# Banded attention and a gated MLP on one core: values of two head pairs in one place, a load moved behind stores, a third row buffer

## The chip, the cores and the metric

The kernel runs on one core of a Trainium2 chip. The metric is the device time of one execution in microseconds. Three runs of the kernel before took 677.02, 677.27 and 681.09 us; the median is 677.27. Engine names follow the profile: PE is TensorE (PEld its weight loads), DVE is VectorE, ACT is ScalarE, POOL is GpSimd, SP is SyncE, which here only issues DMAs.

## What is computed

```python
def _attn_ref(q, k, v, n_global, n_local):          # q, k, v: (4, 8, 768, 64) float32
    scores = np.matmul(q, k.transpose(0, 1, 3, 2)) / np.sqrt(D)
    rel = pos[:, None] - pos[None, :]
    is_global = pos[None, :] < n_global             # 8
    is_local = (rel >= 0) & (rel < n_local)         # 96
    dist = np.where(is_global & ~is_local, float(n_local), np.abs(rel))
    scores = scores - slopes[:, None, None] * dist  # one slope per head
    scores = np.where(is_global | is_local, scores, -1e9)
    a = softmax(scores)
    return np.matmul(a, v)

def _moe_ref(x, w_in, w_out):                       # x: the attention's output, (3072, 512); w_in (512, 2048)
    h = x @ w_in
    return (h * np.clip(h + 3.0, 0.0, 6.0) / 6.0) @ w_out
```

Each query sees at most 96 local and 8 global keys, so only a band of the scores is ever computed. All is float32 at float32 accuracy: the large products are made of three products of rounded parts (high by high, low by high, high by low).

## The kernel before, in words

The 3072 rows are eight **blocks** of 384 rows (4 batches by two halves of the sequence), each of three row tiles of 128. For each block the attention of 8 heads is made in four **pairs** of heads, and then the MLP: for each of 16 slices f of the hidden layer a first product (`first`, L164, 12 matmuls into a PSUM bank `hp`), the gate (L175 on ACT, L176 on DVE), its split into a high part `gh` (L182 on POOL) and a low part `gl` (L189 on DVE), and a second product (`second`, L196, 9 matmuls into three banks `acc`). PE alternates between the two, so a slice is two **half-steps** of some 2.1 us each; `halves` (L430) hands control back after each, and the caller then puts the attention's work of that half-step in between.

Blocks 0 and 1 are made in an earlier stage, in which the weights are decoded too. From block 2 on there is the main loop (L549): while block i goes through the MLP, the attention of block i + 1 is made, by a list of `units`, one per half-step, which `attention` (L577) writes out. For pair p, from unit 6p on, it holds:

- units 0 to 2: `scores` of the three row tiles (L767, four matmuls each into a bank `sp` or `tp` in turn; then DVE L774 and ACT's exponential L778);
- unit 3: the sums (L786, L787), and `normalize` of two tiles on POOL (L796); unit 4: the third tile;
- units 4 and 5: `spread`, which transposes on DVE (L821) and stores to a DRAM tile `there` (L823), and `fetch`, which reads that back as the tile `weights` (L830);
- units 3 to 5: `split` of the next pair's queries and keys into rounded parts: `q1` on ACT (L740), `kx` on POOL (L741) and on DVE (L747), `q2` on DVE (L744). Its step 2 ends with a load of a later pair's keys and queries (`load_next`, L295);
- unit 11, thus five half-steps behind the next pair's first scores: `values` (L848), 24 or 20 matmuls of 64 columns into a bank `xp`, a copy and a subtraction out of it (L150 on ACT, L151 on DVE) into the block's x, and a load of a later pair's values.

In block 2, the first of the main loop, all units stand one half-step later, and the first pair (12) is split ahead of the loop; the load that this split ends with stands on SP between the stores of block 0 and those of block 1.

After a block's last slice, `store` (L50) copies the three accumulators on ACT into tiles `o` (L53) and stores each (L54 on SP). The pool of `o` has two tiles in the main loop. Block 1's accumulators are the banks named sp, tp and xp.

Order: the instructions of PE, SP and POOL are held to the order of the program (`in_order`, L567); on ACT and DVE the framework's own scheduler sets the order.

Of the kernel before, what the change touches and what calls it, by code (L numbers as in the profile page):

```python
# [21 lines left out]
TB = NT * P  # L22
# [34 lines left out]
class Kernel:  # L57
# [229 lines left out]
    def load(self, n, values):  # L287


        if n < len(self.blocks) * NPAIR:  # L290
            parts = [(slice(KW + QW, LOAD), slice(None))] if values else [(slice(0, KW + QW), slice(None))]
            if n < EARLY and not values:
                parts = [(slice(0, KW), slice(None))] + [(slice(KW + j * TB, KW + (j + 1) * TB), slice(j * D, (j + 1) * D)) for j in range(2)]
            for columns, rows in parts:
                self.nc.sync.dma_start(out=self.place(n)[rows, columns], in_=self.pairs[n, rows, columns])  # L295

    def load_next(self, n, values):

        if n < EARLY - MORE + ROOMS:
            self.load(n + MORE, values)  # L300
        elif n >= EARLY:
            self.load(n + ROOMS, values)
# [155 lines left out]
    def banded(self, flag):  # L458
# [11 lines left out]
        with ExitStack() as early, ExitStack() as words:  # L470
# [14 lines left out]
            with ExitStack() as ctx:  # L485
# [7 lines left out]
                pairs = [Pair(self, n, xs[n // NPAIR], True) for n in range(EARLY)]  # L493
# [46 lines left out]
            todo += [(i, f, xs[i], (acc, acc1)[i]) for f in range(FIRST, NF) for i in range(2)]  # L540
            for _ in self.halves(todo):
                pass
        self.attending(self.ctx, 2, 3, 1, side="right")
        self.bp = self.pool("bp", 2, side="right")
        self.there = self.pool("there", 2, bass.MemoryType.DRAM)
        self.score_banks = 2
        self.op = self.pool("op", 2, side="right")
        x, ahead = xs[2], None
        for i in range(2, len(self.blocks)):  # L549
            units, x_next = [], None  # L550
            if i + 1 < len(self.blocks):
                x_next = self.x_tiles()
                units, ahead = self.attention(i + 1, x_next, ahead)
                if i == 2:
                    units = [[]] + units
            else:
                units = [[]] * 4 + [[lambda: self.doubt(flag)]]
# [4 lines left out]
            x = x_next  # L562
# [14 lines left out]
    def attention(self, i, x, first):  # L577

        units = [[] for _ in range(2 * NF - 2)]
        pairs = [first or Pair(self, i * NPAIR, x, False)]  # L580
        pairs[0].x = x
        if first is None:
            for k in range(3):
                pairs[0].split(k)
        for p in range(NPAIR):
            n = i * NPAIR + p
            me, after = pairs[p], Pair(self, n + 1, x, False) if n + 1 < len(self.blocks) * NPAIR else None
            pairs.append(after)
            at = units[6 * p:]
            for t in range(NT):  # L590
                at[t].append(lambda t=t, me=me: me.scores(t))
            at[3] += [me.sum_up, lambda me=me: me.normalize(0), lambda me=me: me.normalize(1)]
            at[4] += [lambda me=me: me.normalize(2), lambda me=me: me.spread(0)]
            at[5] += [lambda me=me: me.spread(1), lambda me=me: me.spread(2), me.fetch]
            for t in range(NT if after else 0):
                at[t + 3].append(lambda t=t, after=after: after.split(t))
            at[11].append(me.values)
        return units, pairs[NPAIR]


# [110 lines left out]
class Pair:  # L711
# [11 lines left out]
    def low(self, t):  # L723
        return CB if self.tb == 0 and t == 0 else 0

    def split(self, step):


        nc, kk = self.nc, self.k
        k, q, _, _ = kk.loaded(self.n)  # L730
        c = slice(CB if self.tb == 0 else 0, None)
        for j, part in enumerate(self.parts):
            h = 2 * self.pr + j
            scale = float(-1.0 / (np.sqrt(D) * SLOPES[h]))
            own, other = (slice(0, D), slice(D, P)) if j == 0 else (slice(D, P), slice(0, D))
            if step == 0:
                part["q1"] = kk.hp.tile([P, NT, P], F32R, name="q1")
                part["q2"] = kk.hp.tile([P, NT, P], F32R, name="q2")
                part["kx"] = kk.hp.tile([P, KW], F32R, name="kx")
                nc.scalar.mul(out=part["q1"], in_=q[:, j], mul=scale)  # L740
                nc.gpsimd.tensor_scalar(out=part["kx"][own, c], in0=k[own, c], scalar1=1.0, scalar2=0.0,  # L741
                                        op0=ALU.mult, op1=ALU.add)
            elif step == 1:
                nc.vector.scalar_tensor_tensor(out=part["q2"], in0=q[:, j], scalar=scale, in1=part["q1"].bitcast(F32),  # L744
                                               op0=ALU.mult, op1=ALU.subtract)
            else:
                nc.vector.tensor_tensor(out=part["kx"][other, c], in0=k[own, c], in1=part["kx"][own, c].bitcast(F32),  # L747
                                        op=ALU.subtract)
        if step == 2:
            kk.load_next(self.n, False)  # L750

    def scores(self, t):
# [83 lines left out]
            return self.pts[t][0:K, j, c, :]  # L836
        return self.weights[0:K, :, t, 1 - c, j]

    def values(self):
        nc, kk = self.nc, self.k  # L840
        _, _, va, vb = kk.loaded(self.n)
        xps = kk.bank("x")[:, 0:TB]
        for t in range(NT):
            two = not self.low(t)
            for c in range(2 if two else 1):
                for j in range(2):
                    vt, K = (va, P) if c == 0 else (vb, CB)
                    nc.tensor.matmul(xps[j * D:(j + 1) * D, t * P:(t + 1) * P], lhsT=vt[0:K, t, j * D:(j + 1) * D],  # L848
                                     rhs=self.part(t, j, c, K), start=(c == 0), stop=(c == 1 or not two))
        kk.put_x(self.x, self.pr, xps)  # L850
        kk.load_next(self.n, True)
# [74 lines left out]
```

## Time and profile before

| | |
|---|---|
| three runs, us | 677.02, 677.27, 681.09 |
| profiled execution, us | 678.77 |
| its span, first to last instruction, us | 677.0 |
| mean granted PE clock | 0.995 |
| half-clock stretches of PE after the start | 226.70 to 230.10 us, and the end |
| block 2 of the main loop | about 209 to 288 us |
| values matmuls in the main loop | 448, from 239.3 to 597.6 us |
| bytes moved | 84.33 MB, 125 GB/s on average |

Times of rows are counted from the span's start. A timeline row gives start and length in us, the engine, the line, the operation, what it writes and reads, how many instructions were merged, and in brackets the engine's idle time before it and who ended it. A row of the chain gives start, length and instruction of the chain of waits that ended last. Matmuls overlap: a chain row counts a matmul group from the end of the one before, and a timeline row from its own start, about 0.16 us earlier. A wait for several semaphores is put down to the one that came last by the profile, which can be the wrong one.

### The profile page before, as it was taken

Reading aid. Unit: us, or ns where it says so; the run is one execution under the profiler, and the core shown is the slowest. Engines: PE = TensorE matmul, PEld = TensorE weight load, DVE = VectorE, ACT = ScalarE, POOL = GpSimd, SP = SyncE. Lnnn points to the kernel's source line nnn. Section 1 sums busy time; section 2 is a strip of 40 time slices with the busy share of each in tenths; the row PEclk is TensorE's granted clock in tenths of the full one; section 3 lists DMA queues with packets and bytes.
Section 4 is the critical chain, followed back from the end, with each engine's and each line's share of the span. In section 5 each row is a group of like instructions: output and inputs, shape, how many; then the busy total and the mean of one; then the engine's idle time right before and its main releaser. Section 6 shows DMA issues by size and latency. Waiting matters only on the chain.

```text
span 677.0 us, 11351 instructions
## 1 busy us (share of the span) xinstructions
PE 659.9 (97%) x3905; PEld 589.1 (87%) x3905; DVE 438.5 (65%) x1186; ACT 283.1 (42%) x744; POOL 191.9 (28%) x354
## 2 busy tenths in 40 slices
PE   6999999999999899999999999999999999999996
PEld 5788889999988898898888989898888999889995
DVE  8799999999964667457653676547662676422221
ACT  6998755454545333144332543143331444221111
POOL 2864500000000344233331344315431343302110
PEclk9999999999999899999999999999999999999999
DMA  8677443333303455625553367524564265410001
GB/s 264 176 237 232 140 137 105 109 110 107 112 0 132 132 155 157 160 90 154 142 159 97 103 167 205 156 71 125 142 166 128 80 171 138 107 45 18 1 1 51
DMA packets 62611, 84.33 MB, mean 125 GB/s; under 512 B 8784, under 2 KB 48720, under 8 KB 62544
## 3 DMA queue, kind: packets, MB, share of 16 engines
q1 hardware_dynamic: 62256, 83.25, 42.1%
q8 instruction: 33, 0.54, 0.3%
q14 instruction: 34, 0.28, 0.1%
q10 hardware_dynamic: 288, 0.26, 0.1%
HBM read 62.52 MB, written 20.97 MB: 123 GB/s over the span
## 4 chain that ended last, share of the span: by engine, by line
PE 88%; DVE 3%; ACT 3%; DMA 2%; POOL 2%; issue 1%; SPq 0%; POOLq 0%; ACTq 0%; DVEq 0%
PE hp L164 38%; PE acc L196 32%; PE xp L848 5%; DMA wst<-w 2%; PE sp L767 2%; PE tp L767 2%; POOL n L796 2%; PE sp L196 2%; PE tp L196 2%; PE xp L196 2%; ACT n L778 1%; PE acc L763 1%; PE sp L763 1%; PE acc L848 1%; DVE g L176 0%
## 5 line engine op out<-in xcount | busy, mean ns | idle before, releaser
L164 PE MATMUL hp<-xh,w1h 128*128 128x384 f32 x512 | 175.5, 343 | 0.0
L164 PE MATMUL hp<-xh,w1l 128*128 128x384 f32 x512 | 173.5, 339 | 0.0
L175 ACT ACTIVATE g<-hp,small 128x384 f32<-128x384 f32 x127 | 73.7, 580 | 238.2 <-PE hp L164 226.6
L164 PE MATMUL hp<-xl,w1h 128*128 128x384 f32 x512 | 172.6, 337 | 0.0
L182 POOL TENSOR_SCALAR gh<-g 128x384 fp32r<-128x384 f32 x96 | 57.7, 601 | 300.7 <-DVE g L176 274.9
L196 PE MATMUL acc<-w2h,gl 128*128 128x512 f32 x336 | 132.8, 395 | 0.2
L196 PE MATMUL acc<-w2l,gh 128*128 128x512 f32 x336 | 132.9, 396 | 0.0
L196 PE MATMUL acc<-w2h,gh 128*128 128x512 f32 x336 | 132.5, 394 | 0.3 <-POOL gh L182 0.3
L176 DVE SCALAR_TENSOR_TENSOR g<-g,hp 128x384 f32<-128x384 f32 x128 | 70.4, 550 | 83.3 <-ACT g L175 82.8
L796 POOL TENSOR_SCALAR n<-n,sums 128x232 f32<-128x232 f32 (+1 forms) x186 | 104.3, 576 | 51.0 <-DVE sums L787 41.9
L778 ACT ACTIVATE n<-n,least 128x232 f32<-128x232 f32 (+1 forms) x192 | 89.7, 470 | 43.2 <-DVE least L774 42.1
L189 DVE TENSOR_TENSOR gl<-g,gh 128x384 fp32r<-128x384 f32 x128 | 73.2, 572 | 45.6 <-POOL gh L182 43.9
L164 PEld LDWEIGHTS hp<-xh,w1h 128*128 128x128 f32 x512 | 96.8, 189 | 6.5 <-issue 2.9
L164 PEld LDWEIGHTS hp<-xl,w1h 128*128 128x128 f32 x512 | 96.7, 189 | 3.5
L164 PEld LDWEIGHTS hp<-xh,w1l 128*128 128x128 f32 x512 | 96.5, 188 | 0.0
L196 PEld LDWEIGHTS acc<-w2l,gh 128*128 128x128 f32 x336 | 63.0, 188 | 13.4
L196 PEld LDWEIGHTS acc<-w2h,gh 128*128 128x128 f32 x336 | 63.4, 189 | 11.6 <-POOL gh L182 0.9
L196 PEld LDWEIGHTS acc<-w2h,gl 128*128 128x128 f32 x336 | 63.2, 188 | 11.3 <-DVE gl L189 1.1
L821 DVE STREAM_TRANSPOSE blocks<-n 128x256 f32<-128x256 f32 x112 | 43.5, 424 | 25.5 <-POOL n L796 25.0
L741 POOL TENSOR_SCALAR kx<-load 64x504 fp32r<-64x504 f32 (+1 forms) x40 | 22.9, 573 | 119.2 <-PE hp L164 117.5
L774 DVE CUSTOM_DVE_ANT_0 n<-sp,d 128x232 f32<-128x232 f32 (+1 forms) x60 | 20.7, 382 | 31.1 <-PE sp L767 30.8
L778 ACT ACTIVATION_READ_ACCUMULATOR n<-n,least 128x1 f32 x192 | 36.9, 192 | 0.0
(107 smaller groups left out, 769.3 us busy)
## 6 DMA issues: line engine op xcount, KB each, us to landing
wst<-w SPq DMA_DIRECT2D x32, 512.0 KB, 3.5
there<-blocks SPq DMA_DIRECT2D x52, 256.0 KB, 2.9
load<-pairs SPq DMA_DIRECT2D x20, 636.0 KB, 5.2
load<-pairs SPq DMA_DIRECT2D x32, 384.0 KB, 3.4
weights<-there SPq DMA_DIRECT2D x48, 192.0 KB, 3.6
out<-o SPq DMA_DIRECT2D x23, 256.0 KB, 2.1
weights<-there SPq DMA_DIRECT2D x32, 160.0 KB, 3.2
load<-pairs SPq DMA_DIRECT2D x12, 252.0 KB, 4.1
```

The lines of the kernel that those rows point to most:

```text
L164: self.nc.tensor.matmul(hp, lhsT=self.w1(w, f)[:, kt, :], rhs=a[:, kt, :], start=(n == 0), stop=(n == 3 * NKT - 1))
L175: nc.scalar.activation(out=g, in_=hp, func=AF.Relu, bias=self.three, scale=1.0)
L176: nc.vector.scalar_tensor_tensor(out=g, in0=g, scalar=6.0, in1=hp, op0=ALU.min, op1=ALU.mult)
L182: self.nc.gpsimd.tensor_scalar(out=gh, in0=g, scalar1=1.0, scalar2=0.0, op0=ALU.mult, op1=ALU.add)
L189: self.nc.vector.tensor_tensor(out=gl, in0=g, in1=gh.bitcast(F32), op=ALU.subtract)
L196: self.nc.tensor.matmul(acc[tt], lhsT=a[:, tk], rhs=self.w2(w, f), start=(f == 0 and j == 0), stop=(f == NF - 1 and j == 2))
L741: nc.gpsimd.tensor_scalar(out=part["kx"][own, c], in0=k[own, c], scalar1=1.0, scalar2=0.0, op0=ALU.mult, op1=ALU.add)
L767: nc.tensor.matmul(sp[:, j, lo:W], lhsT=q[:, t], rhs=part["kx"][:, c], start=(m == 0), stop=(m == 1))
L778: nc.scalar.activation(out=e[:, j, lo:W], in_=e[:, j, lo:W], func=AF.Exp, bias=self.least[:, i:i + 1], scale=-1.0, accum_out=self.sums[:, ...
L796: nc.gpsimd.tensor_scalar(out=e[:, j, lo:W], in0=e[:, j, lo:W], scalar1=over, scalar2=0.0, op0=ALU.mult, op1=ALU.add)
L821: nc.vector.transpose(out=blocks[:, :, s].rearrange("p b j q -> p j b q"), in_=e[:, :, c:c + P].rearrange("p j (b q) -> p j b q", b=4))
L848: nc.tensor.matmul(xps[j * D:(j + 1) * D, t * P:(t + 1) * P], lhsT=vt[0:K, t, j * D:(j + 1) * D], rhs=self.part(t, j, c, K), start=(c == 0 ...
```

## The change

Four things change together. The values of two pairs are made in one half-step, one behind the other: those of pairs 0 and 1 at unit 17, those of pairs 2 and 3 at unit 29 (before: units 11, 17, 23 and 29). The second of the two uses one of the score banks, and the pool of fetched weights has two tiles. The load that followed the first pair's split ahead of the loop is issued from unit 1 of the list, which is behind the stores of block 1. The pool of `o` in the main loop has three tiles. The scratch that is set aside in each partition for descriptors of DMAs issued by POOL is set to 1024 bytes.

```diff
-        self.attending(self.ctx, 2, 3, 1, side="right")
+        self.attending(self.ctx, 2, 3, 2, side="right")
...
-        self.op = self.pool("op", 2, side="right")
+        self.op = self.pool("op", 3, side="right")
...
         if first is None:
             for k in range(3):
-                pairs[0].split(k)
+                pairs[0].split(k, False)
+            units[1].append(lambda: self.load_next(pairs[0].n, False))
...
             for t in range(NT if after else 0):
                 at[t + 3].append(lambda t=t, after=after: after.split(t))
-            at[11].append(me.values)
+            if p % 2 == 1:
+                at[11] += [lambda me=pairs[p - 1]: me.values("x"), lambda me=me: me.values("s")]
         return units, pairs[NPAIR]
...
-    def split(self, step):
+    def split(self, step, load=True):
...
-        if step == 2:
+        if step == 2 and load:
             kk.load_next(self.n, False)
...
-    def values(self):
+    def values(self, bank="x"):
         nc, kk = self.nc, self.k
         _, _, va, vb = kk.loaded(self.n)
-        xps = kk.bank("x")[:, 0:TB]
+        xps = kk.bank(bank)[:, 0:TB]
...
-    nc = bacc.Bacc("TRN2", target_bir_lowering=False, num_devices=1)
+    nc = bacc.Bacc("TRN2", target_bir_lowering=False, num_devices=1, dynamic_dma_scratch_size=1024)
```

## The prediction

> **What bounds the kernel now.** I read the page first, then PE's waits, then the chain of waits around each place where PE stood still.
>
> ```profile
> span 677.0 us, 11351 instructions
> PE 88%; DVE 3%; ACT 3%; DMA 2%; POOL 2%; issue 1%; SPq 0%; POOLq 0%; ACTq 0%; DVEq 0%
> PE tp L767 <- DVE kx L747: 1.7, 2, 0.9
> ```
>
> PE sets the end: 88% of the chain. From 100 us on it idles in one place only, the 1.7 us of the last row. So the change can gain in two ways: by shortening what PE issues, and by repairing that place. It lies at the start of the third block (the first of the main loop):
>
> ```profile
> 208.24 0.69 PE xp L196 x3
> 209.37 2.09 PE hp L164 x12
> 214.00 0.46 PE sp L767 x4
> 226.45 3.52 PE hp L164 x12
> 229.97 0.57 PE sp L767 x4
> 230.54 2.09 PE acc L196 x9
> ```
>
> From the end of the scores at 214.46 to 230.54 are 16.08 us. The work there is three hp groups (2.11 each elsewhere), two acc groups (2.08) and two score groups (0.44): 11.37. The loss is **4.7 us**. ACT shows where it starts, and the SP and DMA views why (SP: start, length; DMA: median us to landing):
>
> ```profile
> 214.53 0.60 ACT L53 ACTIVATE o<-xp 128x512 f32<-128x512 f32 x1 [3.57 <-PE sp L767]
> 215.02 0.58 ACT L175 ACTIVATE g<-hp,small 128x384 f32<-128x384 f32 x1
> 207.22 0.38 SPq L295 DMA_DIRECT2D load<-pairs  x1
> 208.20 7.28 SPq L54 DMA_DIRECT2D out<-o  x3
> 222.71 4.48 SPq L823 DMA_DIRECT2D there<-blocks  x3
> load<-pairs SPq DMA_DIRECT2D x20, 636.0 KB, 5.2
> out<-o SPq DMA_DIRECT2D x2, 256.0 KB, 6.2
> out<-o SPq DMA_DIRECT2D x23, 256.0 KB, 2.1
> ```
>
> The third row block of block 1 (o<-xp) was complete on PE at 208.24 + 0.69 = 208.93, yet ACT copied it at 214.53. The PE named as releaser is not what o needs. There are two o buffers, so the third copy waits for the first store, issued at 208.20. That store and the next landed after 6.2 us (208.20 + 6.2 = 214.4), against 2.1 for stores in general, because a 636 KB load went out 1 us before them. Behind the copy, on ACT, stood the gate g, whose hp had been complete since 209.37 + 2.09 = 211.46. The delay reaches PE like this:
>
> ```profile
> 216.90 0.49 PE L196 MATMUL acc<-w2h,gh 128*128 128x512 f32 x1 [0.34 <-POOL gh L182]
> 224.69 0.46 PE L767 MATMUL tp<-kx,q 128*128 128x232 f32 x2 [0.90 <-DVE kx L747]
> 225.16 0.68 DVE L747 TENSOR_TENSOR kx<-load,kx 64x504 fp32r<-64x504 f32 x1
> 225.99 0.46 PE L767 MATMUL tp<-kx,q 128*128 128x232 f32 x2 [0.84 <-DVE kx L747]
> 13.69 0.33 PE L804 MATMUL hp<-ident,n 128*128 128x128 f32 x1 [1.45 <-DVE n L794]
> 11.70:15.10 3.40, 1.95 (x11) 1.00 1.05 341
> 223.30:226.70 3.40, 1.66 (x10) 1.00 0.54 154
> 226.70:230.10 3.40, 3.40 (x13) 0.50 0.28 77
> ```
>
> The last three rows are PE's windows (length, PE busy, granted clock, DMA). After 3.4 us with PE busy for 1.66, the clock was 0.50 for the next 3.4 us: 3.52 instead of 2.11 for one hp group and 0.57 instead of 0.44 for one score group, 1.5 of the 4.7.
>
> **Part 1: load behind the stores, three rows.** The copy o<-xp finds a free buffer whatever the stores do, so ACT's 3.57 us wait goes; the stores no longer follow the load, so they should land near 2.1 us too. On SP the load moves past three stores and issues near 210 instead of 207.2. Nothing is due on SP until the first `there` store at 222.71, and pair 14's keys are first split eight half-steps behind (2.08 us or more each), over 16 us for a landing of 5.2. Its cost is nothing; its cover is those 12 us of an idle queue. The 1024-byte scratch costs nothing either: no DMA is issued from POOL, and it only makes room for the 2 KB row and the second 6 KB `weights` tile per partition.
>
> Not all 4.7 us come back. The scores of the next pair need kx, and that comes late in this block even without ACT's stall, as the next pair of the same block shows:
>
> ```profile
> 235.19 2.08 PE acc L196 x9
> 237.27 2.11 PE hp L164 x12
> 239.38 1.47 PE xp L848 x24
> 240.85 2.28 PE acc L196 x9
> 241.71 0.68 DVE L747 TENSOR_TENSOR kx<-load,kx 64x504 fp32r<-64x504 f32 x1
> 242.97 0.60 PE L767 MATMUL sp<-kx,q 128*128 128x232 f32 x4
> ```
>
> Hp ended at 235.19, kx at 242.39: 7.20 us through ACT g, DVE g, POOL gh, four normalizations and kx. At the stalled pair hp ended at 214.46 + 2.11 = 216.57, so kx would end at 223.77; a matmul starts 0.15 after its kx (225.84 to 225.99), at 223.92. Of the 4.7, 1.54 fell behind 225.99, hence 3.17 ahead of it; without any loss the second head's matmuls would start at 222.82. **A wait of 1.1 us stays**, and Part 1 is worth 4.7 - 1.1 = 3.6. PE would be busy for 2.3 of 3.4 us there; 1.95 (the row 11.70:15.10, with a 1.45 us gap) still kept clock 1.00, so I count no halved clock.
>
> **Part 2: values of two pairs together.** The matmuls are the same, 448 in five blocks. What goes are the edges of a group:
>
> ```profile
> L848 PE MATMUL xp<-weights,load x448: 269/273/324, 239.3 to 597.6; 128*64 128x128 f32 x81, 104*64 104x128 f32 x69
> 314.17 2.09 PE acc L196 x9
> 316.26 1.25 PE xp L848 x20
> 317.50 2.29 PE hp L164 x12
> 322.75 2.11 PE hp L164 x12
> ```
>
> A group of 24 takes 1.47, one of 20 takes 1.25: 0.055 per matmul, so 20 of them explain 1.10 and 0.15 is edge. The group behind takes 2.29 instead of 2.11 (or 2.28 instead of 2.08): 0.19 more. Together 0.34 per group. Twenty groups become ten: 10 x 0.34 = **3.4 us**. The change inside a double group, from one pair's last 104-row matmul to the next pair's first of 128 rows, is a kind that occurs within every group already; no row shows the joint itself, so the bounds are 0 and, with 0.01 of rounding on either term, 0.36 per join, 0 to 3.6, and I take 3.4, since the steps within a group are the nearest rows.
>
> The price: the first pair's values leave their old place, and PE comes to the third pair's scores sooner. In the third block that is 1.47 + 0.20 = 1.67 sooner. Now the second head starts at 242.97 + 0.21 = 243.18, and kx allows 242.39 + 0.15 = 242.54: slack 0.64. So **a new wait of 1.0 us** appears, with the second head's matmuls, scores' bank and all that PE holds behind them moved by it. In the four later blocks the pair before has no values ahead of its scores already, and shows how it goes:
>
> ```profile
> 302.21 1.36 DVE L747 TENSOR_TENSOR kx<-load,kx 64x400 fp32r<-64x400 f32 x2
> 304.32 0.56 PE L767 MATMUL tp<-kx,q 128*128 128x128 f32 x4
> 380.38 1.62 DVE L747 TENSOR_TENSOR kx<-load,kx 64x504 fp32r<-64x504 f32 x2
> 382.32 0.61 PE L767 MATMUL tp<-kx,q 128*128 128x232 f32 x4
> ```
>
> The second kx ends at 303.57 and 382.00, and its matmuls start about 0.2 behind the first head's (304.5, 382.5): with the 0.15, slack of 0.8 and 0.4. No wait there; if that cover goes, each us that kx is later costs one.
>
> The rest is hidden. Two copies out of PSUM instead of one stand on ACT and DVE, but PE has at least one acc group before the next block reads the last pair's part, in its last three matmuls. The second pair's bank is one of the two score banks, needed again by the second score group behind it, over 4 us later. Both value loads now stand on SP ahead of two `there` stores and a fetch, held until PE ends the double group (1.3 us later than one); that fetch serves values that are now 12 half-steps off instead of 6. The odd pairs' fetches stand behind no value load any more. The fetched weights have two tiles, so none waits for the old values to be read.
>
> Sum, against the profiled execution's own 678.77 us (span 677.0 and 1.8 around it): 678.77 - 4.7 + 1.1 + 1.0 - 3.4 = **672.8 us**. The median shown is 677.27. The halved window costs 3.4 / 2 = 1.7 us, and 678.77 - 1.7 = 677.1 is where two of the three runs lie; I take it that these lacked it. Then the stage loses 3.0 in them, and the forecast is the same.
>
> **A rule on the clock.** The row: 1.74 us idle in two pieces within 3.4 us halved the clock, 1.45 in one piece did not. [...]
>
> **The rivals.**
> - *Waits that halve the clock.* One or both of the 1.0 to 1.1 us waits trip it: 1.7 each, 674.5 to 676.2. For: the threshold lies somewhere between 1.45 and 1.74 idle, not far off. Against: 1.1 is below both.
> - *No waits.* The order of DVE's work puts both kx ahead of g (0.56) or frees more: 672.8 - 2.1 = 670.7. For: the order on DVE is the scheduler's own, and in the later blocks the same chain leaves slack. Against: POOL's order is written out, and its gh and normalizations fix most of the 7.20.
> - *The edges stay.* The second pair's matmuls start a group of their own (another bank, another wait): 672.8 + 3.4 = 676.2.
> - *The stores change nothing.* If ACT waited for something other than the buffer, the 3.6 us stay: 676.4. Against: 208.20 + 6.2 fits to 0.1.
> - *Slower.* In the later blocks kx comes behind the gl and the transposes on DVE, as their new order could place it, and PE, now 1.4 to 1.7 us sooner at the third pair's scores, waits there. It decides from a lateness of 1.5 to 1.9 us on (slack 0.4 to 0.8, then four waits of 1.1 that eat the 4.5 us to the median). With gl (0.7) and two pairs of transposes (0.77 each) ahead, waits of up to 1.7 that halve the clock too: 4 x (1.7 + 1.7) = 13.6, 686.4. Against: the pair before has that slack in the later blocks.
>
> **How the numbers follow.** The forecast has 0.58, the halved clock 0.12, no waits 0.13, the edges 0.08, the stores 0.05, slower 0.04. The range reaches from both savings at their upper bound without waits (678.77 - 4.7 - 3.6 = 670.5, and 0.2 for what the rows round) to the edges kept (676.2): 670.3 to 676.2. One per cent, about what a measurement of this kernel can tell from no change, is 6.8 us: faster than 670.5 takes half of "no waits" and a little of the forecast, 0.11; slower is its rival, 0.04; the rest 0.85.
>
> **What would show it.** Right: o<-xp on ACT near 209; the load behind three stores on SP; x48 and x40 values groups, ten in all, with one 2.29 hp group behind each; one PE wait for kx near 223 and one near 236, each about 1 us, at clock 1.00; no kx wait behind 290. Wrong: 0.34 us missing per join, a clock of 0.5 between 220 and 245, or kx waits in the later blocks.

## The result, and the profile after

The changed kernel took 674.77 us (median of 14 runs, 673.90 to 677.62), the kernel before 679.27 us (14 runs, 676.44 to 681.09). The ratio is 0.9944 with a 95% interval of 0.9930 to 0.9958. The forecast was 672.8 within 670.3 to 676.2, with a chance of 0.85 for a change of less than 1%.

The page of the kernel after:

```profile
span 673.1 us, 11323 instructions
PE 87%; DMA 4%; ACT 4%; DVE 2%; POOL 2%; issue 1%; SPq 0%; POOLq 0%; ACTq 0%
```

PE still sets the end (87% of the chain), and the 3.9 us between the two spans can be placed. PE's windows, cut at the first product of block 2, of block 3 and of the last block (length, PE busy, granted clock, DMA share, GB/s), first of before, then of after:

```profile
0.00:204.58 204.58, 194.93 (x1192) 1.00 0.44 143
204.58:288.33 83.75, 81.58 (x482) 0.98 0.55 151
288.33:602.09 313.76, 313.76 (x1889) 1.00 0.47 130
602.09:677.00 74.91, 69.68 (x347) 0.98 0.06 23
```

```profile
0.00:206.17 206.17, 195.30 (x1192) 1.00 0.46 142
206.17:286.71 80.54, 78.85 (x481) 1.00 0.56 156
286.71:598.23 311.52, 311.52 (x1890) 1.00 0.48 131
598.23:673.10 74.87, 69.68 (x347) 0.98 0.06 23
```

The early stage, which the change does not touch, is 1.6 us longer in this execution. Block 2, counted from its first product (at 204.58 in before, not 209 as in the table of times), is 3.2 us shorter, the four blocks behind it together 2.2 us, the last one is the same. From block 2 on that is 5.5 us.

Now the place of the stall, at the start of block 2. All rows are of after. ACT's timeline:

```profile
210.55 0.60 ACT L53 ACTIVATE o<-xp 128x512 f32<-128x512 f32 x1
213.15 0.58 ACT L175 ACTIVATE g<-hp,small 128x384 f32<-128x384 f32 x1 [0.60 <-PE hp L164]
```

SP's timeline (the last store of block 0 and the three of block 1, then the load):

```profile
208.36 3.15 SPq L54 DMA_DIRECT2D out<-o  x4
211.61 1.60 SPq L295 DMA_DIRECT2D load<-pairs  x1
```

The DMA view of block 1's first store (the last number is the time from issue to landing), and PE's timeline at the scores of the second and the third pair:

```profile
out<-o SPq DMA_DIRECT2D x1, 256.0 KB, 2.3
```

```profile
225.51 0.46 PE L769 MATMUL tp<-kx,q 128*128 128x232 f32 x2 [0.84 <-DVE kx L749]
240.53 0.46 PE L769 MATMUL sp<-kx,q 128*128 128x232 f32 x2 [0.84 <-DVE kx L749]
```

The third copy follows the second at once (the row block was complete at 210.52), and the gate starts when its product ends, 2.6 us behind the copy's start. The load stands behind the stores, and the first of them lands after 2.3 us, not 6.2. What is left is one wait of 0.84 for the second head's kx at the second pair, and one like it at the third pair, both as forecast. At both, kx ends 7.2 us behind the end of its product (218.16 to 225.37, 233.17 to 240.39), the time that the prediction worked with. The product and the second head's kx of each, in the chain of waits of after:

```profile
216.03 2.13 PE hp L164 x12
224.68 0.69 DVE kx L749
231.04 2.13 PE hp L164 x12
239.70 0.69 DVE kx L749
```

The joined values in the chain of waits of after:

```profile
252.36 1.47 PE xp L850 x24
253.83 1.32 PE tp L850 x24
255.15 2.28 PE acc L196 x9
```

The groups by line in the main loop (count, busy us, mean ns):

```profile
L850 PE MATMUL xp<-weights,load 128*64 128x128 f32 (+1 forms) x224 | 14.5, 276 | 0.0
L850 PE MATMUL tp<-weights,load 128*64 128x128 f32 (+1 forms) x224 | 14.0, 271 | 0.0
```

The first pair's 24 take 1.47 us as before. The second pair's take 1.32 (24 x 0.055), with no edge of their own, and one longer group follows where there were two.

### The profile page after: what moved, and what is told of

Read it like the earlier page. It is cut to its first block, busy times and chain, and to the rows that moved or that the text cites. A ratio compares the mean times of both kernels' runs of the same rounds, so it can differ in the third digit from the quotient of the medians.

```text
span 673.1 us, 11323 instructions
## 1 busy us (share of the span) xinstructions
PE 655.3 (97%) x3905; PEld 588.5 (87%) x3905; DVE 438.3 (65%) x1186; ACT 283.0 (42%) x744; POOL 192.9 (29%) x354
## 4 chain that ended last, share of the span: by engine, by line
PE 87%; DMA 4%; ACT 4%; DVE 2%; POOL 2%; issue 1%; SPq 0%; POOLq 0%; ACTq 0%
PE hp L164 38%; PE acc L196 32%; DMA wst<-w 4%; PE xp L850 2%; PE sp L769 2%; PE tp L850 2%; PE sp L196 2%; PE tp L196 2%; PE xp L196 2%; PE tp L769 2%; ACT n L780 2%; POOL n L798 1%; PE acc L765 1%; ACT pt L810 1%; PE acc L850 1%
## 5 line engine op out<-in xcount | busy, mean ns | idle before, releaser
L176 DVE SCALAR_TENSOR_TENSOR g<-g,hp 128x384 f32<-128x384 f32 x128 | 70.2, 548 | 76.4 <-ACT g L175 75.9
L776 DVE CUSTOM_DVE_ANT_0 n<-sp,d 128x232 f32<-128x232 f32 (+1 forms) x70 | 23.7, 376 | 37.1 <-PE sp L769 36.8
```

Of the source, the lines that this page charges most:

```text
L176: nc.vector.scalar_tensor_tensor(out=g, in0=g, scalar=6.0, in1=hp, op0=ALU.min, op1=ALU.mult)
L776: nc.vector.tensor_tensor_reduce(out=e[:, j, lo:W], in0=sp[:, j, lo:W], in1=d, op0=ALU.add, op1=ALU.min, scale=scale, scalar=3.0e38, accum ...
```

## The experiments

All runs of this section but the last (e7) are single executions with a profile. Since the early stage differs from execution to execution (below), they are compared by the **main loop**, from the first product of block 2 to the end of the span, and by its blocks. Each length is the difference between the starts of the first `hp` matmuls of two blocks in that run's trace. The last column is the time from issue to landing of the first store of block 1.

| run | block 2 starts | main loop | block 2 | blocks 3 to 6 | last block | store landed after |
|---|---|---|---|---|---|---|
| before | 204.58 | 472.39 | 83.75 | 78.00, 78.88, 78.00, 78.88 | 74.88 | 6.2 |
| after | 206.17 | 466.93 | 80.55 | 77.50, 78.29, 77.51, 78.21 | 74.87 | 2.3 |
| r1_before | 206.79 | 472.58 | 83.69 | 78.00, 78.87, 78.00, 78.87 | 75.15 | 6.2 |
| r2_before | 206.28 | 472.98 | 83.83 | 78.00, 78.87, 78.00, 78.87 | 75.42 | 6.2 |
| e0_scratch | 207.71 | 469.69 | 80.91 | 78.00, 78.88, 78.00, 78.87 | 75.03 | 4.9 |
| e1_part1 | 208.13 | 468.71 | 80.12 | 78.00, 78.88, 78.00, 78.87 | 74.84 | 2.4 |
| e2_part2 | 206.01 | 469.73 | 82.87 | 77.49, 78.29, 77.50, 78.22 | 75.35 | 6.5 |
| e3_rows | 205.85 | 467.43 | 80.52 | 77.49, 78.29, 77.50, 78.26 | 75.37 | 4.9 |
| e4_load | 207.44 | 467.12 | 80.52 | 77.50, 78.31, 77.49, 78.24 | 75.06 | 2.3 |
| e5_shift | 206.41 | 465.24 | 78.60 | 77.50, 78.32, 77.49, 78.25 | 75.08 | 2.0 |
| e6_late | 206.98 | 466.76 | 80.58 | 77.33, 78.22, 77.33, 78.22 | 75.08 | 2.4 |
| e7_both | 205.96 | 464.89 | 78.60 | 77.34, 78.23, 77.33, 78.44 | 74.95 | 2.0 |

The theory that was tested is the prediction's: local terms that add. Rivals were that the tiles' places in SBUF matter, that the two parts depend on each other, and that the waits for kx come from the block's load rather than from how its units stand to the products.

**e1_part1: the first part alone.** Against the kernel after:

```diff
-        self.attending(self.ctx, 2, 3, 2, side="right")
+        self.attending(self.ctx, 2, 3, 1, side="right")
...
-            if p % 2 == 1:
-                at[11] += [lambda me=pairs[p - 1]: me.values("x"), lambda me=me: me.values("s")]
+            at[11].append(me.values)
```

> The change without joined values: load behind the stores, three rows, small scratch, values of each pair in its old place. Theory: only the loss at the third block goes, but for the wait for kx at its second pair (1.1 us), and the third pair's kx wait does not appear: main loop 472.4 - 3.6 = 468.8 us, one wait of 0.84 for kx, clock 1.00. Rival (the waits at the third block belong to the joined values): no wait for kx at all, 467.7.

Measured: 468.71, one wait for kx of 0.84, clock 1.00 in the main loop. Block 2 was 3.63 us shorter than in before, the other blocks were the same within 0.04. Against that execution the first part is worth 3.6 us by itself, and the wait for kx at the second pair belongs to the block and not to the joined values.

**e2_part2: the second part alone.** Against the kernel after:

```diff
-        self.op = self.pool("op", 3, side="right")
+        self.op = self.pool("op", 2, side="right")
...
-                pairs[0].split(k, False)
-            units[1].append(lambda: self.load_next(pairs[0].n, False))
+                pairs[0].split(k)
```

> The change without its first part: joined values and two tiles of fetched weights, but the load ahead of block 1's stores and two rows. Theory: ten joins at 0.34 give 3.4 us, the third pair's kx wait costs 1.1 and late gl in the later blocks 0.4, the stall stays: main loop 472.4 - 3.4 + 1.1 + 0.4 = 470.5 us, 1.7 less if the clock is not halved this time. Rival (the stall and the joins are not additive, the late third block hides the kx wait): 469.4.

Measured: 469.73, against 470.5 less 1.7, since the clock was not halved here (below). The 0.9 above that are a later landing of the store (0.3), a longer last block (0.5), and a halved window that is 1.54 in the prediction's rows and not 1.7. Blocks 3 to 6 are as after. PE's rows at the third block show the old stall and the new wait side by side:

```profile
218.61 0.50 PE L196 MATMUL acc<-w2h,gh 128*128 128x512 f32 x1 [0.62 <-POOL gh L182]
226.39 0.46 PE L768 MATMUL tp<-kx,q 128*128 128x232 f32 x2 [0.89 <-DVE kx L748]
227.69 0.46 PE L768 MATMUL tp<-kx,q 128*128 128x232 f32 x2 [0.84 <-DVE kx L748]
242.69 0.46 PE L768 MATMUL sp<-kx,q 128*128 128x232 f32 x2 [0.84 <-DVE kx L748]
```

The parts add; neither hides the other. From before's block 2, without the halved clock, with the later landing, the new wait (1.11, worked out below) and two joins, come 83.75 - 1.54 + 0.3 + 1.11 - 0.68 = 82.94; measured were 82.87.

**e3_rows and e4_load: the two halves of the first part.** e3 keeps three rows and puts the load back ahead of the stores (the second hunk of e2's diff); e4 moves the load and goes back to two rows (its first hunk).

> The whole change, but the load stays ahead of block 1's stores. Theory (a free third row alone ends ACT's wait): main loop 466.9 us as in the whole change, the stores land after 6 us and nobody waits for them. Rival (the load itself delays the block): 469 to 470.5.

> The whole change with two rows instead of three. Theory (moving the load alone suffices, as the first store then lands after some 2.1 us, at about 1.5 us behind the end of the second copy): ACT waits some 1.5 us for the row, the gate's product is not yet complete by then, and the main loop is 466.9 us. Rival (the third row is needed): 468 to 470.5.

Measured: block 2 took 80.52 us in both, as after (80.55). Their main loops of 467.43 and 467.12 differ from the 466.9 by the last block only. In e3 the first store still landed late, and nobody waited for it. ACT's rows, then the landing of that store in the DMA view, both of e3:

```profile
209.54 0.60 ACT L53 ACTIVATE o<-tp 128x512 f32<-128x512 f32 x1
210.23 0.60 ACT L53 ACTIVATE o<-xp 128x512 f32<-128x512 f32 x1
```

```profile
out<-o SPq DMA_DIRECT2D x1, 256.0 KB, 4.9
```

In e4 the third copy waited for its row and stood behind the exponentials, and the gate followed it without a loss to PE (ACT's timeline of e4):

```profile
213.72 0.57 ACT L53 ACTIVATE o<-xp 128x512 f32<-128x512 f32 x1
214.41 0.58 ACT L175 ACTIVATE g<-hp,small 128x384 f32<-128x384 f32 x1
```

So, within the whole change, either edit alone is worth the whole first part. That ACT waited for a buffer (e3's third copy started at 210.23, right behind the second, with the load still ahead), and that the load ahead of the store held it (landings of 4.9 to 6.5 us with the load ahead, 2.0 to 2.4 with it behind), are both shown.

**e0_scratch and two more executions of the kernel before.** e0 is the kernel before with `dynamic_dma_scratch_size=1024` and nothing else; r1_before and r2_before are the kernel before.

> The kernel before with the smaller scratch alone. Measured by the main loop, from the first product of block 2 to the end of the span: 472.4 us before, 466.9 after. Theory (the scratch moves nothing): 472.4 within 0.3, or 1.7 less if no half-clock window falls into it, with the stall of 4.7 us at the third block unchanged. Rival (part of the 5.5 us comes from where tiles lie in SBUF): 471 or less with the stall as before. The start of block 2 was at 204.6 us before and at 206.2 after; if the scratch set that, it is at 206.2 here, if it is the spread of the early stage, anywhere from 203 to 208.

> The kernel before once more, unchanged, for its profile. Theory (the loss at the third block differs from execution to execution, with the landing of the first store behind the load and with whether PE's idle time falls into one clock window; the early stage spreads by some 3.5 us): third block between 80.5 and 83.8 us long, its length following the landing of that store one for one, plus 1.5 if the clock halves; block 2 starts anywhere from 204 to 208.5. Rival (the smaller scratch cut the loss in the run with the scratch alone): 83 to 84 again, with a landing of 6.2.

> The kernel before a second time, unchanged, for its profile: the same expectations as of the first of these two.

Measured: r1 and r2 repeat the first profile (83.69 and 83.83); e0 has a block 2 of 80.91 with the old stall in it, only shorter. At first sight the rival holds. What differs is the landing of one store, and one clock window. The DMA view of that store, and PE's windows over the two waits for kx and behind them, of r1_before:

```profile
out<-o SPq DMA_DIRECT2D x1, 256.0 KB, 6.2
```

```profile
225.33:228.74 3.41, 1.69 (x9) 1.00 0.53 154
228.74:232.15 3.41, 3.41 (x13) 0.50 0.26 77
```

The same of e0_scratch:

```profile
out<-o SPq DMA_DIRECT2D x1, 256.0 KB, 4.9
```

```profile
225.07:228.48 3.41, 2.01 (x11) 1.00 0.53 154
228.48:231.89 3.41, 3.41 (x21) 1.00 0.26 77
```

The store landed 1.3 us sooner, and the clock was not halved, which the prediction priced at 1.54: 1.3 + 1.54 = 2.84, and the blocks differ by 83.75 - 80.91 = 2.84. The scratch by itself does not fix the landing: with the small scratch and the load in its old place it took 4.9 (e0), 4.9 (e3) and 6.5 us (e2). That six landings of 4.9 to 6.5 are chance alone is not shown; before had 6.2 three times. Nor is the small scratch needed for the clock to hold: five of eleven later runs of the kernel before have a mean granted clock of 0.999 or 1.000, which leaves no room for a halved window (see "The sum").

**e5_shift: the waits for kx.** Against the kernel after:

```diff
-                    units = [[]] + units
+                    units = [[], []] + units[:28] + [units[29]]
```

> The whole change with the third block's units two half-steps late instead of one, so that scores follow first products there as in the later blocks; its last values move one half-step up. Theory (the two waits for kx come from the half-step's parity, kx taking 7.2 us from the end of a product): both 1.1 us waits go, main loop 466.9 - 2.2 = 464.7 us. Rival (they come from the first main block's own load on DVE and POOL): waits stay, 466.9 or more.

Measured: both waits went, and block 2 fell from 80.55 to 78.60, by 1.95 (2.2 were expected); the main loop's 465.24 has 0.2 more in the last block. Block 2's attention and MLP are the same work as before, so it is how the units stand to the products, and not the load on DVE and POOL, that made kx late. Through which step it does so was not tried, but the traces point to POOL's gh, which stands ahead of the normalizations. In after the sums are ready at 218.05, and POOL begins the normalizations at 220.09, behind a gh that waited for the gate (L176 on DVE); in e5 they begin 0.16 us behind the sums. The sums on DVE and POOL's rows of after, then the normalizations of e5:

```profile
217.86 0.19 DVE L789 RECIPROCAL sums<-sums 128x6 f32<-128x6 f32 x1
219.59 0.51 POOL L182 TENSOR_SCALAR gh<-g 128x384 fp32r<-128x384 f32 x1 [4.20 <-DVE g L176]
220.09 2.17 POOL L798 TENSOR_SCALAR n<-n,sums 128x232 f32<-128x232 f32 x4
221.78 1.78 POOL L798 TENSOR_SCALAR n<-n,sums 128x232 f32<-128x232 f32 x4 [1.34 <-DVE sums L789]
```

**e6_late and e7_both.** e6 against the kernel after; e7 has this edit and that of e5:

```diff
-                at[t + 3].append(lambda t=t, after=after: after.split(t))
+                at[t + (3 if p < NPAIR - 1 else 6)].append(lambda t=t, after=after: after.split(t))
```

> The whole change with the split of the next block's first pair three half-steps later. Theory (in the later blocks gl stands on DVE behind that split's kx, and lost its cover when the second-last values left): the 0.1 to 0.2 us in one second product of each later block go, main loop 466.9 - 0.4 = 466.5 us. Rival (the gl is late for another reason): 466.9.

> The whole change with both further edits, the units of the third block two half-steps late and the later split. Theory: the gains add, main loop 466.9 - 2.2 - 0.4 = 464.3 us, some 7 us and 1.0 to 1.1 % below the kernel before by the median. Rival (the moved split takes cover from another step): over 465.

Measured: in e6 blocks 3 to 6 fell by 0.17, 0.07, 0.18 and not at all: 0.4 in sum, as expected. The main loop as a whole was 466.76, between the two expectations, since the last block took 0.2 longer there. What the edit removes, on PE and then on DVE in the kernel after:

```profile
346.87 0.40 PE L196 MATMUL acc<-w2h,gh 128*128 128x512 f32 x1
347.18 0.50 PE L196 MATMUL acc<-w2h,gl 128*128 128x512 f32 x1
```

```profile
345.52 0.87 DVE L749 TENSOR_TENSOR kx<-load,kx 64x504 fp32r<-64x504 f32 x1
346.42 0.70 DVE L189 TENSOR_TENSOR gl<-g,gh 128x384 fp32r<-128x384 f32 x1
```

gl ends at 347.12 behind kx, and PE needed it at 347.10: a matmul starts 0.31 behind its forerunner instead of 0.23, and the next one (at 347.52) 0.34 behind that. e7's main loop was 464.89, where 464.3 was expected, with a new 0.14 us wait at block 2's last values and 0.2 us more in block 6, whose cause is open. It took 672.70 us (median of 6 runs, 672.28 to 674.55) against 679.46 for the kernel before (11 runs): 0.9914 with an interval of 0.9890 to 0.9937. That is 0.9% less, where 1.0 to 1.1% was expected. It is the lowest time and the shortest main loop of these kernels, but its interval still overlaps that of the change (0.9930 to 0.9958).

## Why the prediction was right, point by point

**What bounds.** Right: the stall's cause (a row buffer held by a store that was held by a load) is shown by e3 and e4, each of which removes one of the two and with it all that the first part was to gain.

**Part 1, 3.6 us.** Right: 3.63 in e1. The wait of 1.1 that stays was there, too: e1's one wait. In after it ended at 225.51; the prediction's 223.92, with block 2 starting 1.59 later, is the same. But the 3.6 is not a constant. It fell to 0.8 against e0's execution (80.91 to 80.12), where the store landed sooner and the clock held. The prediction took one execution's stall for the stall.

**Part 2, 0.34 per join.** Right to a hundredth: 48 matmuls take 1.47 + 1.32, and one 2.28 group follows; in e6 each of the blocks 3 to 6, with two joins, is 0.66 to 0.67 shorter than in before. The price at the third pair of block 2 was 80.55 - (80.12 - 0.68) = 1.11, forecast 1.0. The place given for that wait, near 236, was a slip: the prediction's own 243.18, less 3.6 and 1.67, is 237.9, and with block 2 starting 1.6 later 239.5; the wait lay at 239.69 to 240.53.

**What was missed.** "No wait there" in the later blocks held for kx, but not for gl, the next on DVE. The third pair's values leave their old place as well, at unit 23, where the next block's first pair is split. PE comes 1.4 to 1.7 us sooner to the second product behind them, and gl, which stands on DVE behind that split's kx, comes late enough to cost 0.1 to 0.2 us a block: 0.4 us over three blocks, which e6 gives back. The fourth (block 6) has no next block to split for. The step that failed is "The rest is hidden": the prediction priced only the first pair's values leaving, and read the slack there for kx alone.

**The sum.** From block 2 on: -3.2 in it (forecast -4.7 + 1.1 + 1.0 - 0.7 = -3.3) and -2.2 in the four behind (forecast -2.7). In absolute time 672.8 was 2.0 too low. 1.6 us of that is the base: block 2 started at 204.58 in the execution that the sum was made against, the earliest of twelve, whose median is 206.3. Another 0.5 are the four blocks behind block 2. The early stage's spread of 3.5 us over twelve profiles is large beside the spread among the runs (4.7 us before, 3.7 after), and may be most of it.

The prediction read 677.02 and 677.27 as runs without a halved clock. That can't be told from the time alone: e0 without it took 679.2, r1 and r2 with it 681.1 to 681.2. Eleven later runs of the kernel before have their mean granted clock beside the time, and a halved window of 3.41 us in 677 takes 0.0025 from it. The three nearest 677 (676.72, 676.73 and 677.24) have 0.999, so no such window, and the two slowest (680.95 and 681.17) have 0.995. Two with 1.000 and 0.999 took 678.94 and 678.96. So the reading fits, but a run without the halved clock is not always near 677.

The two medians differ by 4.50 us, just what 677.27 less 672.8 gives. That is in part luck: the median of 677.27 came from three runs and that of fourteen is 2.0 higher, and what the first part gains hangs on the landing and the clock of each execution (3.6 us against one profile, 0.8 against another).

**The rivals.** No halved clock at the 1.1 us waits in any of the six profiles that have one: the granted clock over block 2 was 1.00 in after and e6, the mean one was 0.999 in e3 and 1.000 in e1 and e4, and in e2 the first products behind the new wait took 0.34 to 0.35 us a matmul, as elsewhere; no wait for kx in the later blocks; the edges went; the stores counted. "No waits" was 2.1 us away, and e5 shows what it takes.

## What to carry to other kernels

When a copy waits for a buffer, look at what was issued ahead of the store that holds it: a spare buffer or another order of the queue each repaired it (block 2 took 80.52 us with either), and one of them would have done. Work that moves away from a place was also the cover for everything queued behind the next wait there; check each engine's next instruction, not only the one that is late first. Make the sum by stages, and give the stages that the change does not touch their spread from several executions.

## What the runs showed of the hardware

The granted clock was 0.50 from 226.70 to 230.10 us in before and from 228.74 to 232.15 in r1; over the last block its mean was 0.98, in before as in after. PE was not idle in the 3.4 us ahead of the two stretches: it was busy for 1.66 us in before and for 1.69 in r1. In e0 the waits for kx were 0.56 and 0.84 us, PE was busy for 2.01 of the 3.41 us over them, and the clock stayed at 1.00. In e2 the waits were 0.89 and 0.84, nearly those of before (0.90 and 0.84), and the clock stayed at 1.00 as well:

```profile
223.06:226.48 3.42, 2.53 (x13) 1.00 0.23 67
226.48:229.89 3.41, 2.57 (x15) 1.00 0.39 113
```

So whether this stall cost 1.5 us more differed from execution to execution. What decides it is not shown, and neither is a threshold: the 1.45 and 1.74 us of idle time that the prediction read as its two sides are two rows of one profile, and early in e0 PE was busy for only 1.68 us of 3.41, with the clock at 1.00 behind it:

```profile
13.46:16.87 3.41, 1.68 (x10) 1.00 1.06 327
16.87:20.29 3.42, 2.51 (x16) 1.00 0.73 196
```
